# Rows of y regrouped: 64 and 32 rows per pair of heads in place of 32 and 16

## The chip, the cores and the metric

The kernel runs on one NeuronCore of a Trainium2 chip. The metric is the device time of one execution in microseconds (us), as the median of several runs; lower is better. A profiled execution gives a trace beside it, in which each engine's instructions stand with their start and duration.

## What is computed

A linear recurrence over 768 tokens for 4 batches and 8 heads of width 48, then a token mix and a two-layer feed-forward network on the 384 channels.

```python
for t in range(S):                                   # _attn_ref, S = 768, D = 48
    cur = np.einsum('bhd,bhe->bhde', u[None] * kt, vt)
    y[:, :, t] = np.einsum('bhd,bhde->bhe', rt, state + cur)
    state = wt[:, :, :, None] * state + np.einsum('bhd,bhe->bhde', kt, vt)
x = y.transpose(0, 2, 1, 3).reshape(B, S, H * D)     # 384 channels
h = xt @ U @ V                                       # _moe_ref, xt = x with tokens last
u = x + h.transpose(0, 2, 1)
ch = np.maximum(u @ w_ch1, 0.0) @ w_ch2
return u + ch
```

## The kernel before, in words

The 768 tokens of a batch are cut into 6 chunks of 128, so there are 24 chunks, numbered g = 0 to 23, with c = g mod 6 the place in its batch. The 8 heads go in NP = 4 pairs j; head i of a pair has its 48 rows of r and k at partitions 64·i. Per chunk, in float32: `scores` (step AM, line 544) multiplies k by r in products of 64x64 of the TensorE array into `aps`; DVE merges them with a mask into `A` (CP, line 551); `state_add` (DS, lines 560 and 561) builds the change of state `dS`, 48 columns a product; `Z` is the decayed state, 96 columns per pair. Then y, the part that is changed: `y_inner` (YA, lines 622 and 632) multiplies columns of `v` by `A`, and `y_state` (YZ, lines 645 and 649, in the 20 chunks with c > 0) columns of `Z` by the scaled r. All add up in one tile `y` of 128 x 3 x 128 in PSUM, which ScalarE copies to `xT` (XE, line 666). Then come the token mix (`ga`, `gb`, `hp`) and the feed-forward network in blocks of 384 or 512 tokens (UP, line 864, into `hid`; DN, line 898), in float32r.

Rows of y before: the 384 channels are ordered so that the tiles y[:, 0] and y[:, 1] hold the first 32 rows of each of the 8 heads, and y[:, 2] holds the last 16 rows of the 8 heads. The column block of the array in which a product runs is that of the partitions it writes, so a product that writes 32 partitions takes a tile of 128 rows by 32 columns, at column 0, 32, 64 or 96. In `y_inner` that makes 16 products of 32 columns: 8 for the first 32 rows of the heads, at columns 32·(h mod 4), and 8 for the tails, two for each pair at columns 32·j, each with 16 columns of zeros from `v`. In `y_state` there are 12: the 8 heads, and one product per pair for both tails, since `Z` holds both heads of a pair in different rows and a product over all 128 rows gives each its own.

A float32 product is carried out in two passes, so each stands in the trace as two LDWEIGHTS and two MATMUL records; a "record" below is one of these MATMULs. YA and YZ stand next to each other in TensorE's order in all of the 20 chunks that have both.

What sets the order: `ORDER` is a list written out by hand that names every step with its engine, in the order in which it is issued; each engine runs its own steps in that order. The list is not touched by the change, and neither are the buffers.

Of the kernel before, what the change touches and what calls it, by code (L numbers as in the profile page):

```python
# [19 lines left out]
B, H, S, D = 4, 8, 768, 48  # L20
P = 128
NP = H // 2
# [14 lines left out]
HP = P // 2  # L37
NQ = NP // 2
# [9 lines left out]

def channel_order():
    order = []  # L50
    for h in range(H):
        order += [h * D + e for e in range(32)]
    for h in range(H):
        order += [h * D + e for e in range(32, D)]
    return order


# [98 lines left out]
def rwkv_moe_kernel(ctx, tc, wT, rkT, vN, vS, rkN, uB, uT, uD, U, V, w1, w2, out):  # L156
    nc = tc.nc
# [18 lines left out]
    def place(kind, shape, name, buf=None, dtype=F32):  # L176

        n = buf.slot if buf else None
        if n is None:
            n = turns[kind] % slots[kind]  # L180
            turns[kind] += 1
        return homes.get(kind, sb2).tile(shape, dtype, tag=f"{kind}{n}", name=name)
# [15 lines left out]
    def lead(to):  # L198
        if leading[0]:
            warm(leading[0], (to.rearrange("p a b -> p (a b)") if len(to.shape) == 3 else to)[:, 0:TB])  # L200
# [41 lines left out]
    def step(name, eng, fn, after=(), take=(), use=(), alt=None):  # L242

        s = Step(name, eng, fn, after, list(take), list(use), alt)
        steps.append(s)
        return s
# [100 lines left out]
    def chunk(g):  # L347
        b, c = divmod(g, NCH)
# [184 lines left out]
        def scores():  # L533
            rk = st["rk"]
            aps = st["aps"] = aps_all
            lead(aps[:, 0])
            for j in range(NQ):
                for h in range(2):
                    for i in range(2):
                        r = slice(64 * i, 64 * i + D)  # L540
                        for a in range(2):
                            jj, s0 = j + NQ * (a ^ h), HP * h
                            k0 = HP * a
                            nc.tensor.matmul(  # L544
                                aps[HP * a : HP * a + HP, i, jj, s0:P], rk[r, 1, jj, k0 : k0 + HP], rk[r, 0, jj, s0:P],
                                start=True, stop=True,
                            )

        def merge():
            to, new = (t.rearrange("p i j t -> p i (j t)") for t in (st["A"], st["aps"]))  # L550
# [14 lines left out]
        if on:  # L565
# [7 lines left out]
            else:  # L573
                btr = Buf("ffn")
                kt = step("KT " + nm, "PE", turn_k, [ks], take=[btr], use=[buf["rk"]])
                kn = step("KN " + nm, "ACT", copy_k, [kt], take=[buf["kn"]], use=[btr])
        am = step("AM " + nm, "PE", scores, [rp, ks], take=[buf["aps"]], use=[buf["rk"]])
        cp = step("CP " + nm, "DVE", merge, [am] + sel_, use=[buf["aps"], buf["A"]])
        if on:
# [35 lines left out]
        def y_inner():  # L615
            v, A = st["v"], st["A"]
            y = st["y"] = place("y", [P, NCT, P], f"y_{g}", buf["y"])
            lead(y)
            for h in range(H):
                j, i = divmod(h, 2)  # L620
                off = 80 if i else 0
                nc.tensor.matmul(
                    y[32 * (h % 4) : 32 * (h % 4) + 32, h // 4, :],
                    v[:, j, off : off + 32],
                    A[:, i, j, :],
                    start=(h < 4),
                    stop=False,
                )
            for i in range(2):
                for j in range(NP):  # L630
                    off = 48 if i else 32
                    nc.tensor.matmul(
                        y[32 * j : 32 * j + 32, 2, :],
                        v[:, j, off : off + 32],
                        A[:, i, j, :],
                        start=False,
                        stop=c == 0 and i == 1,
                    )

        def y_state():  # L640
            y, Z, rk = st["y"], old["Z"], st["rk"]
            for h in range(H):
                j, i = divmod(h, 2)
                p0 = 32 * (h % 4)
                nc.tensor.matmul(
                    y[p0 : p0 + 32, h // 4, :], Z[:, j, 64 * i : 64 * i + 32], rk[:, 0, j, :], start=False, stop=False
                )
            for j in range(NP):
                nc.tensor.matmul(
                    y[32 * j : 32 * j + 32, 2, :], Z[:, j, 32:64], rk[:, 0, j, :], start=False, stop=True  # L650
                )

        y = step("YA " + nm, "PE", y_inner, [cp, lv], take=[buf["y"]], use=[buf["v"], buf["A"]])
        if c > 0:
            y = step(
                "YZ " + nm, "PE", y_state, [y, rp, old["z"]], use=[buf["y"], old["buf"]["Z"], buf["rk"]]
            )
# [328 lines left out]
    def convert(kind, i):  # L986

        low, high = load_weight(kind, i)
        cols, m = weight_parts(kind, i)[1:]
        a = place("cva", [P, cols], f"cvg_{kind}_{i}")[0:m]  # L990
        to, hi, lo, a_lo, hi_lo = places(kind, i, a)
        ai, e = a.bitcast(U32), low.bitcast(I32)
        nc.scalar.activation(a, high.bitcast(F32), AF.Abs, scale=2.0**16)
        nc.scalar.activation(e, low, AF.Copy, scale=2.0**-29)
        nc.vector.tensor_scalar(
            out=a, in0=a, scalar1=2.0, scalar2=122880.0 * 65536.0, op0=ALU.max, op1=ALU.min
        )
        nc.vector.tensor_scalar(
            out=ai, in0=ai, scalar1=4, scalar2=1, op0=ALU.logical_shift_left, op1=ALU.logical_shift_right
        )  # L1000
        nc.vector.scalar_tensor_tensor(
            out=ai, in0=high, scalar=0x80000000, in1=ai, op0=ALU.bitwise_and, op1=ALU.bitwise_or
        )
        nc.gpsimd.tensor_tensor(out=to.bitcast(I32), in0=a.bitcast(I32), in1=e, op=ALU.add)
        if kind != "U":
            nc.scalar.activation(hi, a, AF.Copy)
            nc.gpsimd.tensor_tensor(out=lo, in0=a_lo, in1=hi_lo.bitcast(F32), op=ALU.subtract)

    def general():
        for key in pieces:  # L1010
            convert(*key)
        xs = dram.tile([B, NP, P, S], F32, name="xs")
        recurrence(xs)
        del steps[:], ups[:]
        with tc.For_i(0, B, 1) as b:
            xb = xs[bass.ds(b, 1)].rearrange("o j p t -> (o p) j t")
            halves = ["g0", "g1"]
            for n, blk in enumerate(halves):
                xT = place("xT", [P, NCT, TB], f"xT_{blk}")
                blocks[blk] = xT  # L1020
                xbuf[blk] = Buf("xT")
                ts = slice(n * TB, (n + 1) * TB)
                for h in range(H):
                    j, i = divmod(h, 2)
                    a0, b0 = (80, 64) if i else (0, 32)
                    p0 = 32 * (h % 4)
                    q0 = 32 * j + 16 * i
                    nc.sync.dma_start(xT[p0 : p0 + 32, h // 4, :], xb[a0 : a0 + 32, j, ts])
                    nc.sync.dma_start(xT[q0 : q0 + 16, 2, :], xb[b0 : b0 + 16, j, ts])
            for c in range(NCH):  # L1030
                n, cc = divmod(c, TB // P)
                turn("g", c, halves[n], cc, [], xbuf[halves[n]])
            token_mix("g")
            to = out[:, :, bass.ds(b, 1)].rearrange("c p o t -> c (p o) t")
            for n, blk in enumerate(halves):
                make_u(blk, [("g", n * TB, TB)], [s for c in range(NCH) for s in xns["g", c]["steps"]])
                ffn(blk, lambda ct, n=n: to[ct, :, n * TB : (n + 1) * TB])
            for s in steps:
                s.run()
# [104 lines left out]
    with tc.If(outside[0] != 0, label="skip", preferred_fallthrough_block=True):  # L1144
        general()
# [79 lines left out]
```

## Time and profile before

| | before |
|---|---|
| median of 3 runs | 434.99 us (434.86 to 435.45) |
| profiled execution, span | 433.5 us |
| TensorE (PE) busy | 418.0 us, 96% |
| VectorE (DVE) busy | 351.0 us, 81% |
| ScalarE (ACT) busy | 185.5 us, 43% |
| GpSimd (POOL) busy | 134.3 us, 31% |
| products of y: lines 622, 632, 645, 649 | 16.8, 15.6, 12.4 and 8.0 us busy, 384, 384, 320 and 160 records |

The span is counted from the first to the last instruction. Busy time of matmuls is a union of overlapping records: each record's end is modelled, and several run side by side in different tiles of the array, so what a product costs is read from the starts of the records, not from their durations. The columns of each view are named where its rows stand; in windows, x counts the records that run in a window, also those begun before it.

### The profile page before, as it was taken

Reading aid. Unit: us, or ns where it says so; the run is one execution under the profiler, and the core shown is the slowest. Engines: PE = TensorE matmul, PEld = TensorE weight load, DVE = VectorE, ACT = ScalarE, POOL = GpSimd, SP = SyncE. Lnnn points to the kernel's source line nnn. Section 1 sums busy time; section 2 is a strip of 40 time slices with the busy share of each in tenths; the row PEclk is TensorE's granted clock in tenths of the full one; section 3 lists DMA queues with packets and bytes.
Section 4 is the critical chain, followed back from the end, with each engine's and each line's share of the span. In section 5 each row is a group of like instructions: output and inputs, shape, how many; then the busy total and the mean of one; then the engine's idle time right before and its main releaser. Section 6 shows DMA issues by size and latency. Waiting matters only on the chain. (4 is left out here: it accounts for less than half of the span.)

```text
span 433.5 us, 10486 instructions
## 1 busy us (share of the span) xinstructions
PE 418.0 (96%) x4156; PEld 363.0 (84%) x4156; DVE 351.0 (81%) x802; ACT 185.5 (43%) x527; POOL 134.3 (31%) x178
## 2 busy tenths in 40 slices
PE   7987999999999999999999999999989999999994
PEld 5976789999998998787778788888767899999994
DVE  8999999998999999999999999999974237325510
ACT  5999889766443343643044254040332012103400
POOL 5665455635735494322238101041000000000000
PEclk9989899999999999999999999999999999999999
DMA  8989638355826464003226403233002041136001
GB/s 279 327 267 338 204 132 310 110 198 172 272 80 217 123 242 158 23 26 107 98 64 231 119 23 117 81 119 122 8 30 74 1 162 39 36 104 206 2 2 60
DMA packets 23913, 57.29 MB, mean 132 GB/s; under 512 B 2864, under 2 KB 7856, under 8 KB 23856
## 3 DMA queue, kind: packets, MB, share of 16 engines
q1 hardware_dynamic: 23856, 56.54, 39.3%
q8 instruction: 34, 0.56, 0.5%
q14 instruction: 23, 0.19, 0.1%
HBM read 51.81 MB, written 4.72 MB: 130 GB/s over the span
## 5 line engine op out<-in xcount | busy, mean ns | idle before, releaser
L898 PE MATMUL f<-hid,w2h 128*128 128x384 f32 (+1 forms) x504 | 148.5, 364 | 0.0
L864 PE MATMUL f<-u,w1h 128*128 128x384 f32 (+1 forms) x504 | 147.8, 364 | 0.6 <-DVE xT L820 0.3
L864 PEld LDWEIGHTS f<-u,w1h 128*128 128x128 f32 x504 | 92.9, 188 | 12.9 <-issue 1.4
L898 PEld LDWEIGHTS f<-hid,w2h 128*128 128x128 f32 x504 | 92.9, 188 | 10.2 <-issue 0.7
L864 PE MATMUL f<-u,w1l 128*128 128x384 f32 (+1 forms) x252 | 90.8, 360 | 0.0
L898 PE MATMUL f<-hid,w2l 128*128 128x384 f32 (+1 forms) x252 | 90.7, 360 | 0.0
L869 ACT ACTIVATE hid<-f 128x384 fp32r<-128x384 f32 (+1 forms) x60 | 32.2, 538 | 96.9 <-PE f L864 88.9
L875 DVE SCALAR_TENSOR_TENSOR hid<-f,hid 128x384 fp32r<-128x384 f32 (+1 forms) x84 | 50.0, 608 | 11.2 <-ACT hid L869 10.5
L898 PEld LDWEIGHTS f<-hid,w2l 128*128 128x128 f32 x252 | 47.4, 188 | 4.7
L864 PEld LDWEIGHTS f<-u,w1l 128*128 128x128 f32 x252 | 47.4, 188 | 4.0
L679 DVE STREAM_TRANSPOSE kn<-rk 32x128 f32<-32x128 f32 x160 | 48.3, 302 | 2.5
L469 ACT ACTIVATE A<-ident,dv 128x128 f32<-128x128 f32 x140 | 43.8, 391 | 6.0 <-DVE dv L455 4.0
L916 DVE TENSOR_TENSOR xT<-f,xT 128x384 f32<-128x384 f32 (+1 forms) x21 | 12.7, 610 | 38.0 <-PE f L898 37.9
L831 POOL TENSOR_TENSOR u<-xT,u 128x512 fp32r<-128x512 f32 (+1 forms) x10 | 12.3, 1238 | 91.5 <-PE f L864 35.8
L322 POOL TENSOR_TENSOR cva_w<-cva_w,raw_w 128x384 int32<-128x384 int32 x24 | 25.0, 1055 | 41.1 <-DVE cva_w L315 15.7
L405 DVE TENSOR_TENSOR_SCAN Q<-w,starts,qd 128x258 f32<-128x258 f32 x48 | 33.3, 735 | 0.5 <-POOL rk L413 0.2
L551 DVE COPY_PREDICATED A<-maskf,aps 128x1024 f32<-128x1024 uint32 x24 | 31.6, 1315 | 0.4 <-PE aps L544 0.2
L390 DVE TENSOR_TENSOR_SCAN F<-w,qd 128x259 f32<-128x259 f32 x48 | 30.4, 675 | 0.5 <-DMA w<-in_wT 0.4
L716 DVE STREAM_TRANSPOSE xn<-xT 32x192 f32<-32x192 f32 x80 | 29.5, 369 | 1.1
L413 POOL TENSOR_TENSOR rk<-rk,Q 128x512 f32<-128x512 f32 x18 | 21.5, 1193 | 25.4 <-DVE Q L405 25.4
L871 DVE TENSOR_SCALAR hid<-f 128x384 fp32r<-128x384 f32 (+1 forms) x24 | 14.3, 596 | 17.7 <-PE f L864 14.4
L475 POOL TENSOR_SCALAR_AFFINE_SELECT A<-dv 128x128 f32<-128x128 f32 (+1 forms) x39 | 11.7, 333 | 43.1 <-DVE dv L455 20.0
(126 smaller groups left out, 568.2 us busy)
## 6 DMA issues: line engine op xcount, KB each, us to landing
raw_w<-in_w SPq DMA_DIRECT2D x48, 384.0 KB, 3.8
rk<-in_rkT SPq DMA_DIRECT2D x24, 512.0 KB, 5.4
kr<-in_rkN SPq DMA_DIRECT2D x18, 384.0 KB, 4.1
w<-in_wT SPq DMA_DIRECT2D x24, 260.0 KB, 4.0
v<-in_vS SPq DMA_DIRECT2D x24, 224.0 KB, 4.6
out_dram<-xT SPq DMA_DIRECT2D x12, 192.0 KB, 3.5
out_dram<-xT SPq DMA_DIRECT2D x9, 256.0 KB, 4.7
raw_V<-in_V SPq DMA_DIRECT2D x8, 96.0 KB, 3.8
```

The source lines that it names most:

```text
L322: lambda: nc.gpsimd.tensor_tensor(out=d["to"].bitcast(I32), in0=d["a"].bitcast(I32), in1=d["e"], op=ALU.add),
L390: nc.vector.tensor_tensor_scan(out=back(F), data0=back(st["w"]), data1=back(qd, OVER * h), initial=1.0, op0=ALU.mult, op1=ALU.add)
L405: nc.vector.tensor_tensor_scan(out=st["Q"][:, a:e], data0=st["w"][:, a:e], data1=qd[:, a - OVER * h : e - OVER * h], initial=starts[:, h : ...
L413: ENG[eng].tensor_tensor(out=rk[:, 0], in0=rk[:, 0], in1=Qv, op=ALU.mult)
L469: nc.scalar.activation(to, one, AF.Copy, scale=dv[:, NP * i + j : NP * i + j + 1])
L551: nc.vector.copy_predicated(to, mask2, new)
L679: nc.vector.transpose(to[32 * j : 32 * j + 32, :, 32 * i : 32 * i + 32], src[32 * i : 32 * i + 32, :, 32 * j : 32 * j + 32])
L716: nc.vector.transpose(to[q, :, :, r], src[r, :, :, q])
L864: nc.tensor.matmul(ps, wt[:, f, ct, :], u[ct][:, z], start=(m == 0), stop=(m == 8))
L869: nc.scalar.activation(h[:, 0], d["ps", f], AF.Relu)
L875: nc.vector.scalar_tensor_tensor(out=h[:, 1], in0=d["ps", f], scalar=0.0, in1=h[:, 0].bitcast(F32), op0=ALU.max, op1=ALU.subtract)
L898: nc.tensor.matmul(d["o", ct], wt[:, 4 * ct + part, f - 3 * part, :], hid[f][:, z], start=(part == 0 and m == 0), stop=(part == 3 and m == 8),
```

## The change

It has three parts. The channels are reordered: y[:, 0] and y[:, 1] now hold, for each pair, 64 rows: the 48 of its first head and the first 16 of its second; y[:, 2] holds the other 32 rows of the four second heads. In `y_inner` a pair has one product of 64 columns for the first head (the last 16 columns are zeros), and two of 32 columns for the second head; the eight of 32 columns run in an order that is written out. In `y_state` a pair has one product of 32 columns and one of 64, the 32s first. The columns of v in DRAM are laid out to match. Last, in `scores` the four loops are run in another order for g = 8, 9 and 10. `general()`, a path for inputs out of range, is changed to match; it is not run here.

```diff
 def channel_order():
     order = []
-    for h in range(H):
-        order += [h * D + e for e in range(32)]
-    for h in range(H):
-        order += [h * D + e for e in range(32, D)]
+    for j in range(NP):
+        order += [2 * j * D + e for e in range(D)] + [(2 * j + 1) * D + e for e in range(16)]
+    for j in range(NP):
+        order += [(2 * j + 1) * D + e for e in range(16, D)]
     return order
...
-            for j in range(NQ):
-                for h in range(2):
-                    for i in range(2):
-                        r = slice(64 * i, 64 * i + D)
-                        for a in range(2):
...
+            two = range(2)
+            tiles = [(j, h, i, a) for j in two for h in two for i in two for a in two]
+            if g == 8:
+                tiles = [(j, h, i, a) for j in two for h in two for a in two for i in two]
+            if g == 9:
+                tiles = [(j, h, i, a) for h in two for j in two for i in two for a in two]
+            if g == 10:
+                tiles = [(j, h, i, a) for i in two for j in two for h in two for a in two]
+            for j, h, i, a in tiles:
...
-            for h in range(H):
-                j, i = divmod(h, 2)
-                off = 80 if i else 0
+            for j in range(NP):
+                p0 = 64 * (j % 2)
+                nc.tensor.matmul(y[p0 : p0 + 64, j // 2, :], v[:, j, 0:64], A[:, 0, j, :], start=j < 2, stop=False)
+            for j, tail in ((0, 0), (1, 0), (0, 1), (2, 1), (2, 0), (3, 0), (1, 1), (3, 1)):
+                p0, ct = (32 * j, 2) if tail else (64 * (j % 2) + 32, j // 2)
+                off = 80 if tail else 48
                 nc.tensor.matmul(
-                    y[32 * (h % 4) : 32 * (h % 4) + 32, h // 4, :],
-                    v[:, j, off : off + 32],
-                    A[:, i, j, :],
-                    start=(h < 4),
-                    stop=False,
+                    y[p0 : p0 + 32, ct, :], v[:, j, off : off + 32], A[:, 1, j, :], start=False, stop=bool(c == 0 and tail)
                 )
-            for i in range(2):
-                for j in range(NP):
-                    off = 48 if i else 32
-                    nc.tensor.matmul(
-                        y[32 * j : 32 * j + 32, 2, :],
...
         def y_state():
             y, Z, rk = st["y"], old["Z"], st["rk"]
-            for h in range(H):
-                j, i = divmod(h, 2)
-                p0 = 32 * (h % 4)
+            for j in range(NP):
                 nc.tensor.matmul(
-                    y[p0 : p0 + 32, h // 4, :], Z[:, j, 64 * i : 64 * i + 32], rk[:, 0, j, :], start=False, stop=False
+                    y[32 * j : 32 * j + 32, 2, :], Z[:, j, 64:96], rk[:, 0, j, :], start=False, stop=False
                 )
             for j in range(NP):
+                p0 = 64 * (j % 2)
                 nc.tensor.matmul(
-                    y[32 * j : 32 * j + 32, 2, :], Z[:, j, 32:64], rk[:, 0, j, :], start=False, stop=True
+                    y[p0 : p0 + 64, j // 2, :], Z[:, j, 0:64], rk[:, 0, j, :], start=False, stop=j >= NQ
                 )
...
-        t[..., 64:80] = vn[:, :, :, 1::2, 32:]
-        t[..., 80:112] = vn[:, :, :, 1::2, :32]
+        t[..., 64:112] = vn[:, :, :, 1::2]
```

## Rows read from the trace of the kernel before

**Rows 1.** The page: span, and its part 1, busy time by engine.
```profile
span 433.5 us, 10486 instructions
PE 418.0 (96%) x4156; PEld 363.0 (84%) x4156; DVE 351.0 (81%) x802; ACT 185.5 (43%) x527; POOL 134.3 (31%) x178
```

**Rows 2.** Windows: stretch, length, busy PE, PEld, DVE, ACT, POOL, granted clock, DMA.
```profile
40.00:50.00 10.00, 7.62 (x182) 6.39 (x183) 9.79 (x18) 8.37 (x26) 5.21 (x6) 0.83 0.69 240
...
300.00:310.00 10.00, 10.00 (x136) 8.43 (x136) 9.72 (x24) 2.63 (x7) 0.00 (x0) 1.00 0.01 2
```

**Rows 3.** The chain that ended last, its passing to TensorE: start, duration, what.
```profile
320.42 0.39 DVE xn L716
320.85 0.58 PE ga L761 x8
...
352.34 6.24 PE f L864 x36
```

**Rows 4.** Timeline of TensorE over one chunk's y (g = 7): start, length, line, operands.
```profile
68.39 0.68 PE L864 MATMUL f<-u,w1h 128*128 128x384 f32 x3
69.01 0.56 PE L561 MATMUL dS<-v,kn 128*48 128x48 f32 x16
69.50 0.64 PE L622 MATMUL y<-A,v 128*32 128x128 f32 x16
69.96 0.62 PE L632 MATMUL y<-A,v 128*32 128x128 f32 x16
70.40 0.62 PE L645 MATMUL y<-rk,Z 128*32 128x128 f32 x16
70.83 0.40 PE L649 MATMUL y<-rk,Z 128*32 128x128 f32 x8
71.17 0.45 PE L815 MATMUL hp<-Vst,gs 96*128 96x384 f32 x1
```

**Rows 5.** Windows, line 622's records alone: PE and PEld running, clock, DMA.
```profile
69.53:69.63 0.10, 0.10 (x4) 0.10 (x8) 1.00 1.06 420
69.63:69.67 0.04, 0.04 (x8) 0.04 (x8) 1.00 0.83 326
```

**Rows 6.** Timeline of TensorE, from the feed-forward network into the scores.
```profile
77.36 0.69 PE L864 MATMUL f<-u,w1h 128*128 128x384 f32 x3
77.98 0.90 PE L544 MATMUL aps<-rk 48*64 48x128 f32 x32
```

**Rows 7.** Windows within the records of these scores, as in Rows 5.
```profile
78.13:78.17 0.04, 0.04 (x8) 0.04 (x8) 1.00 0.76 307
...
78.24:78.28 0.04, 0.04 (x12) 0.04 (x8) 1.00 1.13 461
```

**Rows 8.** Timeline of TensorE, state of g = 1, where lines 560 and 561 alternate.
```profile
23.27 0.30 PE L560 MATMUL dS<-Z,ident 128*48 128x48 f32 x4
23.40 0.27 PE L561 MATMUL dS<-v,kn 128*48 128x48 f32 x4
```

**Rows 9.** Timeline, ScalarE and TensorE, about TensorE's longest wait (in brackets).
```profile
41.18 1.00 ACT L602 ACTIVATE Z<-dS,tots 128x96 f32<-128x96 f32 x4
...
42.24 0.30 PE L560 MATMUL dS<-Z,ident 128*48 128x48 f32 x4 [2.43 <-ACT Z L602]
```

**Rows 10.** TensorE's waits: who for whom, us in total, times, longest.
```profile
PE ga L761 <- DVE xn L716: 1.0, 2, 0.7
...
PE gb L772 <- DVE xT L916: 0.7, 1, 0.7
...
PE f L864 <- DVE xT L820: 0.3, 1, 0.3
PE f L864 <- DVE hid L875: 0.3, 1, 0.3
```

**Rows 11.** Timeline of VectorE at two of its waits for TensorE (in brackets).
```profile
102.41 0.56 DVE L916 TENSOR_TENSOR xT<-f,xT 128x384 f32<-128x384 f32 x1 [1.16 <-PE f L898]
...
150.95 0.69 DVE L820 TENSOR_TENSOR xT<-hp,xT 128x512 f32<-128x512 f32 x1 [0.42 <-PE hp L815]
```

More of the change, by code (lines that the diff above doesn't have):

```diff
@@ L536, in scores @@
             lead(aps[:, 0])
-            for j in range(NQ):
-                for h in range(2):
-                    for i in range(2):
-                        r = slice(64 * i, 64 * i + D)
-                        for a in range(2):
-                            jj, s0 = j + NQ * (a ^ h), HP * h
-                            k0 = HP * a
-                            nc.tensor.matmul(
-                                aps[HP * a : HP * a + HP, i, jj, s0:P], rk[r, 1, jj, k0 : k0 + HP], rk[r, 0, jj, s0:P],
-                                start=True, stop=True,
-                            )
+            two = range(2)
[7 more added lines that the diff above has]
+            for j, h, i, a in tiles:
+                r = slice(64 * i, 64 * i + D)
+                jj, s0 = j + NQ * (a ^ h), HP * h
+                k0 = HP * a
+                nc.tensor.matmul(
+                    aps[HP * a : HP * a + HP, i, jj, s0:P], rk[r, 1, jj, k0 : k0 + HP], rk[r, 0, jj, s0:P],
+                    start=True, stop=True,
+                )
         def merge():
@@ L618, in y_inner @@
             lead(y)
-            for h in range(H):
-                j, i = divmod(h, 2)
-                off = 80 if i else 0
-                nc.tensor.matmul(
-                    y[32 * (h % 4) : 32 * (h % 4) + 32, h // 4, :],
-                    v[:, j, off : off + 32],
-                    A[:, i, j, :],
-                    start=(h < 4),
-                    stop=False,
-                )
-            for i in range(2):
-                for j in range(NP):
-                    off = 48 if i else 32
-                    nc.tensor.matmul(
-                        y[32 * j : 32 * j + 32, 2, :],
[L634 to L638, printed above, removed]
+            for j in range(NP):
[4 more added lines that the diff above has]
+                off = 80 if tail else 48
+                nc.tensor.matmul(
+                    y[p0 : p0 + 32, ct, :], v[:, j, off : off + 32], A[:, 1, j, :], start=False, stop=bool(c == 0 and tail)
+                )
         def y_state():
             y, Z, rk = st["y"], old["Z"], st["rk"]
-            for h in range(H):
-                j, i = divmod(h, 2)
-                p0 = 32 * (h % 4)
+            for j in range(NP):
                 nc.tensor.matmul(
-                    y[p0 : p0 + 32, h // 4, :], Z[:, j, 64 * i : 64 * i + 32], rk[:, 0, j, :], start=False, stop=False
+                    y[32 * j : 32 * j + 32, 2, :], Z[:, j, 64:96], rk[:, 0, j, :], start=False, stop=False
                 )
             for j in range(NP):
+                p0 = 64 * (j % 2)
                 nc.tensor.matmul(
-                    y[32 * j : 32 * j + 32, 2, :], Z[:, j, 32:64], rk[:, 0, j, :], start=False, stop=True
+                    y[p0 : p0 + 64, j // 2, :], Z[:, j, 0:64], rk[:, 0, j, :], start=False, stop=j >= NQ
                 )
@@ L1022, in general @@
                 ts = slice(n * TB, (n + 1) * TB)
[L1023 to L1029, printed above, removed]
+                for j in range(NP):
+                    p0 = 64 * (j % 2)
+                    nc.sync.dma_start(xT[p0 : p0 + D, j // 2, :], xb[0:D, j, ts])
+                    nc.sync.dma_start(xT[p0 + D : p0 + 64, j // 2, :], xb[64:80, j, ts])
+                    nc.sync.dma_start(xT[32 * j : 32 * j + 32, 2, :], xb[80:112, j, ts])
             for c in range(NCH):
```

## The prediction, made before the change was run

> **What bounds the kernel now.** I read the share of busy time first, then the windows along the span, then the chain that ended last, and only then single records. TensorE is busy for 418.0 of 433.5 us [rows 1], but that share mixes stages. The windows separate them: from 300 to 310 us TensorE is at 10.00 of 10 us and VectorE at 9.72 [rows 2], so both are full, each with work in its own order. The chain shows where one of them lets the other go: at 320.85 us the last token mix starts behind VectorE's transposes, and from then on TensorE runs alone to the end, 36 products of the feed-forward network in 6.24 us, 0.173 each [rows 3]. So anything that lengthens TensorE's work before 320.85 us lengthens the time, except where TensorE waits for someone. All work on y lies before that.
>
> What is bought or saved is then read from records of one chunk, TensorE alone. The products of y start at 69.50 us and the next work at 71.17 [rows 4]. In it 16 records take 0.44 us (line 632 to 645) and again 0.43 (645 to 649). That is 27 ns a record, but not an even 27: in the 0.10 us from 69.53 to 69.63 no fifth record joins the first four, and the next four start together [rows 5]. Four records in the four column blocks of the array run side by side, and **a round of four takes 0.109 us**. The unit of cost is therefore the column block in time, not the instruction. 56 records make 14 rounds, 1.53 us; the 0.14 left of 1.67 is 0.02 in the first round (0.46 for the first 16 records against 0.44) and 0.12 at the end, of which about 0.02 is the stagger of the last four.
>
> **A change of the tile's width or height has a price.** Ahead of the state's products three records of the feed-forward network should take 3 x 0.173 = 0.52 us and take 0.62 [rows 3, 4]; ahead of the scores, again 0.62 [rows 6]. So a change costs 0.10 us, to 128x64 as to 64x64, and the 0.12 at the end of y fits. Within y of before there is none, as all its tiles are 128x32. The first round after a change is also longer, since the second pass's weights are not there yet: by 0.02 for 32 columns [rows 4]; for 64 columns the scores start at 77.98, their second four appear about 0.16 later and their third 0.11 after that [rows 6, 7], so 0.05.
>
> **The change, part by part.**
>
> (1) Fewer products. `y_inner` goes from 16 to 12, `y_state` from 12 to 8: 16 records less in each of 20 chunks, 8 less in the other four. By rounds this is worth nothing: a product of 64 columns fills two blocks. In `y_state` 12 x 32 columns become 4 x 32 + 4 x 64, which is 384 columns both times, 6 rounds. In `y_inner` 512 columns stay 512.
>
> (2) Balance. The four products of 64 columns fill all blocks evenly, 4 rounds. The eight of 32 don't: by the code four of them go to partitions 64·(j mod 2) + 32, that is to blocks 32 and 96 only, and four to blocks 0, 32, 64, 96. Blocks 32 and 96 get three products, the others one: 6 rounds where 4 would do. The 32-column products of `y_state` follow in the same tile width, one per block, 2 rounds more on the loaded blocks. So a chunk has 4 + 8 + 4 = 16 rounds against 14: **+0.22 us**, and without `y_state` 10 against 8, the same.
>
> (3) Changes of width. y now runs 64, then 32, then 64 columns wide. Against before: first round 0.05 in place of 0.02 (+0.03); change to 32 (0.10 + 0.02); change back to 64 (0.10 + 0.05). With (2): 0.03 + 0.22 + 0.12 + 0.15 = 0.52 us for each of 20 chunks, and 0.37 for the four without `y_state`. Against this, `dS` has tiles of 128x64 too (two heads at 0 and 64), so where it stands right ahead of y (9 chunks, as at 69.01 [rows 4]) the entry costs nothing, -0.15; where it comes right behind (5 chunks) -0.13. Beside `ga`, which is 32 wide, two changes are new, +0.12 each (g = 12 and 23). Sum: 10.4 + 1.5 - 1.35 - 0.65 + 0.2 = 10.1 us.
>
> (4) The scores of g = 8, 9 and 10. The same tiles get the same work; g = 8 and 9 still have all four tiles in turn. For g = 10 all products of one row half come first, which keep two tiles busy. Whether the other two start beside them depends on how far a waiting product holds up the next. In the state of g = 1 the code issues lines 560 and 561 for one head before the other head's 560, and yet the first four records to start are all of line 560 [rows 8]: a later product overtakes one that waits for its tile, over at least four records. Here it would be sixteen. Bounds: 0 and the whole second half, 0.66 us (4 x 0.109 + 4 x 0.055). I take 0.3. The Trainium skill, "TensorE: Matmul & The Clock Gate", Part 3, says that matmuls start and end strictly in program order; by that the price would be 0.66. The rows speak against it.
>
> (5) The order of channels, v's columns and the weights' rows: the DMAs keep their sizes, ScalarE still copies one 128x384 tile. Nothing. The copy of y to `xT` waits some 0.5 us longer, as does all behind it on TensorE: that is the same time, counted once.
>
> Total on TensorE: **10.4 us** (10.1 to 10.8).
>
> **What of it reaches the end.** Up to g = 3 (1.5 us) it meets TensorE's longest wait, 2.43 us at 42.24 for ScalarE's `Z` [rows 9], and the 40 to 50 us window has TensorE at 7.62 and VectorE at 9.79 [rows 2]: hidden. Without this cover it would cost its 1.5. Behind that TensorE waits before 321 us for VectorE: 1.0, 0.7, 0.3 and 0.3 us [rows 10], 2.3 in all; these can shrink as TensorE comes later, if VectorE does not come later too. But VectorE itself waits for TensorE, 1.16 us at 102.41 and 0.42 at 150.95 [rows 11], so up to there it is pushed along. What TensorE loses behind 151 us (g = 13 to 23: 4.7 us by the same terms) is more than 2.3, so I let those waits take 2.3. That leaves 10.4 - 1.5 - 2.3 = 6.6 us: 440.1 for the profiled span of 433.5. The median shown is 434.99, 1.5 above that span; the same added: 441.5.
>
> **The rivals.**
>
> Records, not rounds, are the cost. 27 ns a record would also fit the 56 of a chunk. Then 20 x 16 + 4 x 8 = 352 records less save TensorE 9.5 us, more than the changes of width cost. VectorE, full until 320.85, would let little through, about what it waits for TensorE [rows 11], 1.6 us: 433.4, **faster**. It decides if 40 records of y take under 1.3 us. The pauses of [rows 5] speak against it. The Trainium skill, "TensorE: Matmul & The Clock Gate", section "Wait — 56ns, not 53.3ns?", gives a floor of about 25 ns from start to start however small the product; by that rule this rival would hold, at 16 x 25 = 0.4 us a chunk. The trace does not agree: four start within 0.04 us.
>
> Only the height of a tile, not its width, forces the 0.10 us while the rows stay 128. Then a chunk costs 0.25 less what `dS` saves, 24 x 0.25 - 2.0 + 0.3 = 4.3, of which 0.6 and 2.3 are absorbed: 436.4. Against it: y's end into `hp`, 32 to 128 columns, costs it [rows 4].
>
> Nothing is absorbed, because VectorE is pushed along everywhere: 434.99 + 10.8 = 445.8.
>
> VectorE covers it all: about 435.0. TensorE's waits, 4.7 us in sum, are too few for it.
>
> The wide products don't run two by two: 8 more rounds in 20 chunks and 4 in four, 19 us: about 461. Against it: four tiles of the scores start together [rows 7].
>
> **How the numbers follow.** Forecast 0.67 (440 to 443.5); nothing absorbed 0.12; height alone 0.08; records 0.07; covered 0.04; not two by two 0.02. The range 436.5 to 446 leaves out the last three, 0.13. A difference of about 0.2% is what a measurement of this kernel can tell from none; above it slower: 0.67 + 0.12 + 0.08 + 0.02 = 0.89; within it 0.04; faster 0.07.
>
> **What would show it.** In the trace of the changed kernel: y of a chunk with state takes about 2.07 us from its first record to the last round's end against 1.55; a step of about 0.20 from the last 64-wide record to the first 32-wide; records of the 32-wide part that start two, not four, at a time; `dS` and the wide products without a gap; the scores of g = 10 longer by up to 0.66; the waits of [rows 10] shorter. I am wrong if y of a chunk is shorter than before, if the change from 64 to 32 columns shows no gap, or if TensorE's waits before 321 us grow.

## The result: 1.4% slower

The changed kernel takes 440.95 us (median of 4 runs, 440.4 to 442.79) against 434.93 before: a ratio of 1.0138, 95% interval 1.0112 to 1.0163. Run once more beside other kernels it gave 1.0126 (1.0103 to 1.0150). 441.5 had been forecast.

The page of the changed kernel, its span, the busy times and the shares of the chain that ended last, by engine:

```profile
span 439.4 us, 9782 instructions
...
PE 426.1 (97%) x3804; PEld 365.6 (83%) x3804; DVE 351.8 (80%) x802; ACT 185.6 (42%) x527; POOL 134.3 (31%) x178
...
PE 86%; ACT 6%; DVE 5%; DMA 1%; issue 0%; POOL 0%; DVEq 0%
```

The span grows by 5.9 us, with 352 records fewer on TensorE (3804 against 4156 of [rows 1]), while its busy time grows by 8.1 us. The other engines' busy times stay. The chain that ended last now runs through TensorE for 86% of the span; before, the part of it that could be followed began at 230 us and was split between TensorE and VectorE.

The y of g = 7 in the changed kernel, TensorE's timeline with the columns of [rows 4]; lines 626 and 642 are the 64-wide products of `y_inner` and `y_state`, 630 and 637 the 32-wide:

```profile
69.39 0.68 PE L857 MATMUL f<-u,w1h 128*128 128x384 f32 x3
70.01 0.56 PE L566 MATMUL dS<-v,kn 128*48 128x48 f32 x16
70.40 0.62 PE L626 MATMUL y<-A,v 128*64 128x128 f32 x8
70.95 0.52 PE L630 MATMUL y<-A,v 128*32 128x128 f32 x10
71.21 0.30 PE L637 MATMUL y<-rk,Z 128*32 128x128 f32 x1
...
71.56 0.47 PE L637 MATMUL y<-rk,Z 128*32 128x128 f32 x5
71.95 0.66 PE L642 MATMUL y<-rk,Z 128*64 128x128 f32 x8
72.54 0.44 PE L808 MATMUL hp<-Vst,gs 96*128 96x384 f32 x1
72.82 0.34 PE L857 MATMUL f<-u,w1h 128*128 128x384 f32 x1
```

From the start of y to the next work 2.14 us against 1.67 in [rows 4], with 40 records for 56. Each piece is where it was forecast. Four rounds of wide products would end at 70.40 + 0.44 = 70.84; the narrow ones start at 70.95, so a change of width costs about 0.1 us though the rows stay 128. The narrow part takes 1.00 us to the wide one's start at 71.95: eight rounds of 0.109, 0.02, and 0.1 for the change. The state's products need 0.39 us to y, not 0.49: from 128x64 to 128x64 nothing is paid. Products of line 637 start before the last of line 630: idle blocks do take the next work, but blocks 32 and 96 have eight rounds whatever happens.

**How the delay builds up.** The products of the feed-forward network are the same 1512 in both traces, in the same order. So the start of the n-th in one trace can be set against the n-th in the other, and each step of the difference belongs to what lies between (us):

| first such product behind | before | changed | lag | step |
|---|---|---|---|---|
| first block's token mix (g = 0 to 6) | 59.46 | 60.47 | 1.01 | +1.01 |
| y of g = 7 (behind `dS`) | 71.45 | 72.82 | 1.37 | +0.37 |
| scores of g = 10 | 112.49 | 114.97 | 2.48 | +0.38 for these scores |
| y of g = 11 (no `dS` beside it) | 134.42 | 137.78 | 3.36 | +0.51 |
| y of g = 13 (`dS` behind it) | 160.30 | 164.55 | 4.25 | +0.37 |
| y of g = 14 | 173.30 | 178.05 | 4.76 | +0.50 |
| TensorE's wait for VectorE's `hid` at 176 us of before | 176.25 | 180.47 | 4.21 | -0.55 |
| y of g = 17 | 204.89 | 210.25 | 5.36 | +0.50 |
| TensorE's waits for VectorE in the token mix at 219 us of before | 219.08 | 223.12 | 4.04 | -1.33 |
| y of g = 23, a 32-wide product behind | 313.71 | 319.92 | 6.21 | +0.64 |
| last token mix | 322.42 | 328.34 | 5.91 | -0.31 |

TensorE's waits in the changed kernel; the columns are those of [rows 10]:

```profile
PE dS L565 <- ACT Z L607: 2.4, 1, 2.4
...
PE aps L549 <- POOL rk L413: 0.9, 1, 0.9
...
PE ga L754 <- DVE xn L709: 0.4, 1, 0.4
```

Of the waits of [rows 10] only 0.4 is left of the 1.0 for `xn`; those of `gb` for `xT`, and of `f` for `xT` and `hid`, are no longer listed. The wait for ScalarE's `Z` (`dS`, 2.43 in [rows 9]) has not shrunk.

### The profile page after: what moved, and what is told of

The parts are those of the page before. It is cut to its first block, busy times and chain, and to the rows that moved or that the text cites. A ratio compares the mean times of both kernels' runs of the same rounds, so it can differ in the third digit from the quotient of the medians.

```text
span 439.4 us, 9782 instructions
## 1 busy us (share of the span) xinstructions
PE 426.1 (97%) x3804; PEld 365.6 (83%) x3804; DVE 351.8 (80%) x802; ACT 185.6 (42%) x527; POOL 134.3 (31%) x178
## 4 chain that ended last, share of the span: by engine, by line
PE 86%; ACT 6%; DVE 5%; DMA 1%; issue 0%; POOL 0%; DVEq 0%
PE f L891 34%; PE f L857 32%; PE aps L549 4%; PE y L630 3%; PE y L626 3%; PE y L642 2%; ACT A L469 2%; PE dS L566 2%; PE trd L496 1%; PE y L637 1%; PE hp L808 1%; DVE kn L672 1%; PE ga L754 1%; ACT Z L607 1%; PE trk L522 1%; DVE hid L868 1%
## 5 line engine op out<-in xcount | busy, mean ns | idle before, releaser
L549 PEld LDWEIGHTS aps<-rk 48*64 48x64 f32 x768 | 21.1, 147 | 5.6 <-issue 3.2
```

Source lines behind the costliest of these rows:

```text
L549: nc.tensor.matmul(aps[HP * a : HP * a + HP, i, jj, s0:P], rk[r, 1, jj, k0 : k0 + HP], rk[r, 0, jj, s0:P], start=True, stop=True,)
```

## The experiments

All run against the kernel before, whose median beside them was 435.3 to 435.6 us. Where 0.5% matters, ratios are given with their 95% interval.

### Uneven blocks without a change of width

```diff
-            for j in range(NP):
-                p0 = 64 * (j % 2)
-                nc.tensor.matmul(y[p0 : p0 + 64, j // 2, :], v[:, j, 0:64], A[:, 0, j, :], start=j < 2, stop=False)
+            for i in range(2):
+                for j in range(NP):
+                    p0 = 64 * (j % 2) + 32 * i
+                    nc.tensor.matmul(
+                        y[p0 : p0 + 32, j // 2, :], v[:, j, 32 * i : 32 * i + 32], A[:, 0, j, :], start=j < 2, stop=False
+                    )
```

(and the same for the wide products of `y_state`).

> The changed kernel with each product of 64 columns cut into two of 32, so that y has 32-wide tiles alone: the uneven column blocks stay, the changes of width go. Theory (a column block's time and the changes of width are the cost): 16 rounds of four against 14 per chunk, no change of width inside y; TensorE +0.22 us in each of 24 chunks and +0.38 for the scores of g = 10, 5.6 us, of which some 0.9 early and 2.3 late are absorbed by TensorE's waits: about 437.3. Rival, records are the cost: 56 records per chunk as before, so about 435. Rival, the changes of width are all of it: 435.

Measured: 437.79 us, 1.0050 (1.0035 to 1.0066). In the same comparison of starts every chunk from g = 7 on is late by 0.22 to 0.25 us, whatever stands beside it, and g = 10's scores add their 0.38. Its y of g = 7, timeline, first lines and next work:

```profile
69.60 0.66 PE L627 MATMUL y<-A,v 128*32 128x128 f32 x16
70.06 0.53 PE L633 MATMUL y<-A,v 128*32 128x128 f32 x10
...
71.50 0.44 PE L812 MATMUL hp<-Vst,gs 96*128 96x384 f32 x1
```

1.90 us against the 1.67 of [rows 4], with the same 56 records: two rounds more. The rival that counts records falls, as does the one that puts everything on the changes of width.

### Even blocks, with the changes of width

The rows of pairs 2 and 3 are mirrored in y, v and Z, and the eight narrow products of `y_inner` are issued in plain order. Two cuts of the edit:

```diff
+        order += one + two if j < NQ else two + one
...
-                p0, ct = (32 * j, 2) if tail else (64 * (j % 2) + 32, j // 2)
+                p0, ct = (32 * j, 2) if tail else (64 * (j % 2) + (0 if j >= NQ else 32), j // 2)
```

> The changed kernel with the rows of pairs 2 and 3 mirrored (16 rows of the second head ahead of the 48 of the first), so that the eight narrow products of y_inner fall two on each column block; the same number of products and of changes of width. Theory: 14 rounds per chunk, y of a chunk with state 1.85 us from its first start to the end of its last round in place of 2.07, TensorE 5.2 us less than in the changed kernel: about 437 to 438. Rival, the changes of width alone are the cost, the uneven blocks are filled by other products: as the changed kernel, 441.

Measured: 439.18 us, 1.0079 (1.0061 to 1.0097). Its y of g = 7, timeline:

```profile
70.98 0.62 PE L629 MATMUL y<-A,v 128*64 128x128 f32 x8
71.53 0.64 PE L633 MATMUL y<-A,v 128*32 128x128 f32 x16
71.99 0.40 PE L640 MATMUL y<-rk,Z 128*32 128x128 f32 x8
72.33 0.66 PE L645 MATMUL y<-rk,Z 128*64 128x128 f32 x8
72.91 0.45 PE L811 MATMUL hp<-Vst,gs 96*128 96x384 f32 x1
```

1.93 us in place of 2.14: the narrow part takes 0.80 to the wide products, not 1.00. Chunks with state are late by 0.16 to 0.17 beside `dS` and 0.29 to 0.30 without (0.44 at g = 23, with its 32-wide product behind), 0.2 less than in the changed kernel, as expected. The time is some 1 us above the 437 to 438 expected. By the ratios it lies 2.6 us under the changed kernel, and the chunks from g = 7 on give 2.4 of that (their lag sums to 2.5 against 4.9), so the early chunks gained next to nothing. Its trace has a lag of 1.58 us before the first feed-forward product, where the kernel with 32 columns alone had 0.11. That stage is taken up below.

### Even blocks, 32 columns alone, old order of the scores

> The rows of y in the mirrored order of the balanced kernel, every product 32 columns wide, the scores in their old order: the regrouped rows without uneven blocks, without changes of width and without the scores' orders. Theory: 14 rounds per chunk, y 1.46 us from first to last start as before, so the time of before within 0.3%. Rival, part of the loss comes from the other layout of rows, weights or v: 436 or more.

The edit is the mirrored rows of the kernel above, with each wide product cut in two, and `tiles` in `scores` as for the other chunks. Measured: 434.99 us, 0.9993 (0.9979 to 1.0007). So regrouped rows, a new layout of v and reordered weights cost nothing in themselves. This was measured with the mirrored rows; with the changed kernel's own rows the first experiment comes nearest, where uneven blocks and scores make up all of the lag behind g = 7. No part of the 1.4% is seen beside uneven blocks, changes of width and scores.

### One change of width in place of two

The 32-wide products of `y_inner` move behind the 64-wide ones of `y_state`. In a first version, for all chunks, the second step also holds the buffers of v and A longer:

```diff
-            for j, tail in (...): 32-wide products of y_inner            # in y_inner
+            narrow()                                                    # in y_state, behind its 64-wide products
...
-                ... use=[buf["y"], old["buf"]["Z"], buf["rk"]]
+                ... use=[buf["y"], old["buf"]["Z"], buf["rk"], buf["v"], buf["A"]]
```

> The changed kernel with the 32-wide products of y_inner issued behind the 64-wide of y_state, beside the narrow ones of y_state: the same products, one change of width within y in place of two. Theory: 0.15 us less in 20 chunks, 0.13 more where the state's products follow (5 chunks): TensorE -2.4 us, about 438.5 to 439. Rival, a change between 64 and 32 columns at 128 rows is free: as the changed kernel, 441.

Measured: 440.23 us, 1.0108 (1.0091 to 1.0125), above the 438.5 to 439 expected. Most chunks do get shorter (0.22 late beside `dS` ahead, 0.35 without or with `dS` behind), but 0.51 us is lost behind g = 9, and g = 10 is late by 0.57. Its trace, of the longest of its six runs (442.58 us), also has a wait for the load of v that is at most 0.8 us in the other kernels' traces:

```profile
PE dS L566 <- DMA v<-in_vS: 2.4, 1, 2.4
```

The longer hold is not what delayed this load. It was issued at 17.73 us, as in the kernel before, and landed at 24.35 in place of 23.13; in the kernel below whose scores go four records per tile, which holds nothing longer, it was issued at 17.82 and landed at 24.48. The second version leaves all buffers as they are, and makes the move only where nothing takes v's and A's in between:

> The changed kernel with one change of width within y in the 12 chunks in which nothing takes the buffers of v and A between the two steps (3, 4, 5, 7 to 10, 13, 19, 20, 22, 23), all buffers as in the changed kernel. Theory: 0.15 us less in seven of them and 0.02 less in the five with the state's products behind, 1.15 us on TensorE; per chunk 0.35 above before where the changed kernel has 0.50: about 440 to 440.5 against 441. Rival, a change between 64 and 32 columns is free: per chunk as the changed kernel.

Measured: 440.25 us, 1.0107 (1.0085 to 1.0130); too near the changed kernel's 1.0138 to tell by time alone. The trace tells it. y of g = 7, where 0.22 us is lost in place of 0.37:

```profile
68.83 0.62 PE L636 MATMUL y<-A,v 128*64 128x128 f32 x8
69.29 0.61 PE L656 MATMUL y<-rk,Z 128*64 128x128 f32 x8
69.82 0.52 PE L626 MATMUL y<-A,v 128*32 128x128 f32 x10
...
70.82 0.44 PE L827 MATMUL hp<-Vst,gs 96*128 96x384 f32 x1
```

The two wide parts follow each other in 0.46 us, a bare four rounds with the first one longer, and one change of 0.1 plus its slow first round is gone: 1.99 us from start to next work, 0.15 less. A change between 64 and 32 columns at 128 rows isn't free. Two places did not gain. Behind g = 9 a transpose waits 0.28 us more for ScalarE's copy of y. And g = 10 is late by 0.57: its second wide part takes 0.75 us to the narrow one, where that of g = 7 takes 0.53. There the weights of the last pair wait for ScalarE: the last piece of `Z` ends at 124.91 us and their load starts at 124.96, 0.17 after its place in the round. A wide part that comes earlier also needs its `Z` earlier.

### The same time on TensorE without any regrouping

```diff
+            for m in range(8):
+                nc.tensor.matmul(
+                    y[32 * (m % 4) : 32 * (m % 4) + 32, 0, :], blank[:, 0:32], A[:, 0, 0, :], start=False, stop=False
+                )
```

> The kernel before with eight more 32-wide products of zero weights in y_inner, two for each column block: four rounds, 0.44 us of TensorE per chunk, no change of width, no other layout, 10.5 us in all, as much as the changed kernel adds. Theory (the time follows TensorE's added time alone, wherever in y it comes from): 441 as the changed kernel, TensorE's waits before 321 us shrinking by the same 2 us and the early part hidden. Rival, part of the changed kernel's loss is from elsewhere (layout, scores, who waits for what): less than 440. Rival, TensorE's added time is mostly covered by VectorE: 436 to 437.

Measured: 441.29 us, 1.0130 (1.0110 to 1.0151), the changed kernel's loss. Each chunk is 0.43 to 0.44 late; the lag falls by 0.55 at 176, 1.23 at 219, 0.43 at 244 and 0.2 at 322 us, the four places of the changed kernel. Its profiled run was the shortest of the six (439.56 us). So the time follows TensorE's added time, wherever in y it comes from.

Split by chunks, with the changed kernel beside:

> The kernel before with the four rounds of zero products (0.44 us of TensorE) in the first seven chunks alone, ahead of the feed-forward network. Theory of the prediction: what g = 0 to 3 adds (1.7 us) is hidden by the 2.43 us wait for ScalarE's Z, what g = 4 to 6 adds (1.3 us) reaches the first product of the feed-forward network, and TensorE's later waits take it up in part: 435 to 436.3. Rival, VectorE and ScalarE alone set the early stage: 435.0. Rival, it all reaches the end: 438.

> The same zero products in chunks 7 to 23 alone: 17 x 0.435 = 7.4 us on TensorE. Theory: TensorE's waits for VectorE before 321 us take 2.4, the rest reaches the end, +5.0: 440.0. Rival, VectorE comes later too and the waits stay: 442.4. Rival, VectorE's full queue covers more of it: under 438.

> The changed kernel once more, on the same chip as the two kernels with zero products: 440.5 to 441.5. With zero products in all chunks the time was 1.3% above before; the changed kernel adds the same on TensorE, so it should lie at the sum of what the early and the late part give, within 0.5 us.

Measured: early chunks alone 436.79 us, 1.0034 (1.0019 to 1.0050); late chunks alone 440.65, 1.0117 (1.0097 to 1.0136); the changed kernel 440.24, 1.0126 (1.0103 to 1.0150). The late part came out as expected: in its trace the lag grows by 17 steps, 7.3 us in sum, and gives 2.5 back at the same four places, +4.9. In its median it is +5.4.

The early part costs 1.5 us, a little above the 0 to 1.3 that I expected. And the two parts did not add up: their sum puts the changed kernel at 442.2, and it came at 440.24, 1.9 below (1.1 by the ratios) where I had said within 0.5; it also lies just under the 440.5 to 441.5 named for it. Zeros in all chunks, at 1.0130, are under that sum as well (1.0151). So the early part isn't known to better than about 1 us.

The zeros in the early chunks, one execution, TensorE's wait for ScalarE's Z, 2.43 in [rows 9]:

```profile
PE dS L560 <- ACT Z L602: 0.5, 1, 0.5
```

In that execution the cover worked: the wait shrank by 1.9 us and the first feed-forward product was 0.14 late. In the changed kernel it did not shrink: it is 2.4 us in the first profile, above, and 3.0 in the second. What is gone from both is a wait for ScalarE's `tots`. First the line of the kernel before, then that of the changed kernel's second profile:

```profile
PE trk L522 <- ACT tots L397: 1.4, 1, 1.4
```

```profile
PE dS L565 <- ACT Z L607: 3.0, 1, 3.0
```

The zeros' 12 runs spread from 435.04 to 438.86, and the profiled one was among the shortest, at 435.33; in the median some 1.5 us come through. The early stage differs from run to run for one and the same kernel. Windows of the changed kernel's first profile and of its second, columns as in [rows 2]:

```profile
10.00:20.00 10.00, 10.00 (x92) 8.96 (x84) 9.86 (x21) 9.35 (x32) 8.01 (x9) 0.50 0.98 325
20.00:30.00 10.00, 10.00 (x173) 8.82 (x174) 10.00 (x23) 9.64 (x33) 6.26 (x7) 0.72 0.83 276
```

```profile
10.00:20.00 10.00, 10.00 (x88) 9.03 (x84) 9.86 (x21) 9.36 (x32) 7.91 (x9) 1.00 0.97 326
20.00:30.00 10.00, 9.92 (x176) 8.44 (x175) 10.00 (x23) 9.64 (x33) 6.26 (x7) 1.00 0.80 258
```

The granted clock was at its lower level (0.50, 1.2 GHz) for ten microseconds and more in the one and at 2.4 GHz in the other, and VectorE did the same work in both. In the first 10 us TensorE had been busy for 6.74 in the one and for 7.88 in the other. The lag at the first feed-forward product was 1.01 us in the one and -0.08 in the other; the steps behind it agree within 0.01, so the difference lasts to the end (5.91 and 4.83) and TensorE's later waits take up none of it.

A lag there in one trace is not the change's alone: the late zeros' kernel, whose first seven chunks are those of before, has 1.03. Four traces had the full clock up to that product (1.00 in every 10 us; the kernel before had 0.94 on average): -0.55 for the even blocks with 32 columns, where nothing is added, -0.48 for zeros in all chunks, 3.0 us added, -0.56 for one change of width in 12 chunks, and -0.08 for the changed kernel. So at the full clock up to 3 us more on TensorE came to at most 0.5 us there. The clock is not all of it: the even-block kernel, with its lag of 1.58, had the full clock except for 0.83 from 40 to 50 us.

### The scores' orders

In the changed kernel the scores of g = 8 and 9 take 0.83 us to the next work, as before; those of g = 10 take 1.21 (113.76 to 114.97). Windows within these, of their records alone, PE and PEld running:

```profile
113.75:114.15 0.40, 0.39 (x9) 0.39 (x11) 1.00 1.08 404
114.15:114.17 0.02, 0.02 (x10) 0.02 (x8) 1.00 0.72 269
```

In the first 0.4 us records start two by two. At 114.14 the two first tiles start the fifth of their eight records, and 13 ns later the first records of the other row half start. So three records were waiting behind the running one in each tile; once the eighth had a place, the products behind were let through. Since two tiles fill by turns here, six waiting in all would look the same as three per tile, and no run tells the two apart.

That reading was tried in all chunks of the kernel before, first with a whole row half ahead (16 records, eight per tile), then with half of one (four per tile):

```diff
-            for j in range(NQ):
-                for h in range(2):
-                    for i in range(2):
+            for j, h, i, a in [(j, h, i, a) for i in two for j in two for h in two for a in two]:   # eight per tile
+            for j, h, i, a in [(j, h, i, a) for j in two for i in two for h in two for a in two]:   # four per tile
```

> The kernel before with the scores' products of one row half all ahead of the other's, in all chunks (the order that the change gives g = 10). In the changed kernel's trace these scores take 1.06 us from first to last start against 0.68, since the second half's first record starts when the first tiles have three records left to start. Theory (a tile holds one running and three waiting records, a product that finds no room holds up all behind it): +0.38 us in each chunk, 9.2 us on TensorE, some 2 early and 2.3 late absorbed: about 440. Rival, strict order of starts: +0.66 per chunk, 15.8 us: 446. Rival, the 0.38 was of that chunk alone: 435.

> The kernel before with the scores' order j, row half, h, a: two products, so four records, for each of two tiles ahead of the two other tiles. Theory (room for four records per tile): the four fit, the other tiles start at once, the scores take 0.68 to 0.72 us from first to last start: the time of before. Rival, room for two records: the second half starts some 0.2 us late, about 0.2 us more per chunk: 436 to 438. Rival, strict order: +0.66 per chunk, 446.

Measured: 440.43 us, 1.0122 (1.0093 to 1.0151) for eight per tile; 435.47, 1.0001 (0.9987 to 1.0015) for four. One chunk's scores in each, timeline, scores and the next work:

```profile
78.20 1.28 PE L542 MATMUL aps<-rk 48*64 48x128 f32 x32
79.41 0.44 PE L862 MATMUL f<-u,w1h 128*128 128x384 f32 x1
```

```profile
80.23 0.95 PE L542 MATMUL aps<-rk 48*64 48x128 f32 x32
81.11 0.45 PE L862 MATMUL f<-u,w1h 128*128 128x384 f32 x1
```

1.21 us against 0.83 before with eight per tile, in every chunk at full clock; 0.88 with four. Strict order would have cost 0.66, full freedom nothing; it is 0.38, and four records per tile nearly fit (0.05). The Trainium skill, "TensorE: Matmul & The Clock Gate", Part 3, has matmuls start in strict program order. Here they start in order within a tile, and the other tiles go ahead as long as the waiting ones have room.

## Why the prediction was right

The time, 441.5, and each term but the early one were near; the terms were:

- A round of four, 0.109 us, as the unit of cost: right. 352 records less brought nothing. The rival by records fell: y with 40 records takes longer than with 56, and cutting the wide products in two made the kernel faster, not slower. With it falls, between tiles, the floor of about 25 ns from start to start that the Trainium skill gives ("TensorE: Matmul & The Clock Gate", section "Wait — 56ns, not 53.3ns?").
- Uneven blocks, +0.22 us a chunk: 0.22 to 0.25 measured, with 32 columns alone.
- Changes of width, 0.10 each plus a slower first round: 0.15 for the one taken away in the 12-chunk experiment, 0.15 forecast. A chunk without `dS` beside it was forecast at 0.52 and costs 0.50; with `dS` ahead 0.37 and 0.37; with `dS` behind 0.39 and 0.37.
- Scores of g = 10: 0.3 taken between 0 and 0.66; 0.38. Those of 8 and 9 nothing, as forecast.
- What TensorE's waits give back behind g = 7: 2.3 forecast, 2.4 measured (0.55, 1.33, 0.21 and 0.31).
- The early chunks are the term that was argued most loosely, and its mechanism was wrong in part. I named one cover, the 2.43 us wait for ScalarE's `Z`; it shrinks in the trace with early zeros, but not in either trace of the changed kernel (2.4 and 3.0), where another wait for ScalarE went. I let 1.5 us be hidden and 1.4 reach the feed-forward network; the lag there was 1.0 and -0.1 in two profiles of the changed kernel, 1.0 in a kernel with nothing added there, and at the full clock 3.0 us of zeros came to under 0.1 us more than nothing added. That 1.4 lies near the 1.0 of the first profile is luck. With 4.9 from the late chunks, 1.0 makes the 5.9 of the profiled execution; the forecast's 6.6 was high by 0.4 there and by 0.3 in the late chunks. The same kernel's second profile, with -0.1, is 4.8 late.

What stays open: how much of the early stage's spread of 1 to 3 us is the clock's and how much is due to when ScalarE and the loads get done; the even-block kernel's lag sits there, and so does the 2.4 us wait for v in the first kernel with one change. No experiment here gives a version faster than before. The wide products save no rounds, and the best regrouped kernel, even and with 32 columns alone, takes the time of before (0.9993).

## What to carry to other kernels

Price small products by how long each column block of the array is occupied, and add the blocks up one by one: fewer and wider instructions are no gain when the same columns stream the same data, and the fullest block sets the time. Keep products of one tile size together, since each change of height or width costs about 0.1 us here, forty times in this kernel. On an engine that hardly waits, such tenths add up nearly undiminished; look for where another engine's wait gives some back, and don't trust a cover seen in one execution of a stage whose clock varies.

## What the runs showed of the hardware

- With two tiles of the array filled by turns, each holds a running record and three waiting ones. A product for another tile overtakes them; one more for a full tile holds up all behind it (0.38 us for eight per tile, 0.05 for four). Whether the room is three per tile or six in all is not shown.
- A change between 128x64 and 128x32 costs the same 0.1 us as one between 128x128 and 64x64, also within one accumulation.
- In the first 50 us one kernel was granted 1.2 GHz for over ten microseconds in one execution and 2.4 GHz in another, and the feed-forward network began 1.1 us later in the first. VectorE and ScalarE were nearly full there at either clock (9.86 and 9.35 of 10 us); that this is why the difference stays so small is my reading, and no run tests it.
